# Order of a product, output stores and operand sums changed in a three-stage attention and feed-forward kernel

## The chip, the core and the metric

The kernel runs on one core of a Trainium2 chip. The metric is the device time of one execution in microseconds, lower is better. The engines of the core are named as in the profile: PE (TensorE; PEld is its weight load), DVE (VectorE), ACT (ScalarE), POOL (GpSimd) and SP (SyncE, which here only issues DMAs).

## The reference

Three stages follow one another; all arithmetic is fp32, and the weights arrive as fp64.

```python
kv  = einsum('bhsd,bhse->bhde', k, v)            # 8 batches, 8 heads, 576 tokens, 64 columns
o   = einsum('bhsd,bhde->bhse', q, kv)
o   = o / sqrt(mean(o * o, -1) + 1e-6) * g_norm
x   = o.transpose(0, 2, 1, 3).reshape(4608, 512)
h   = maximum(maximum(x @ w1, x @ w2), x @ w3)   # 512 x 768 each
x1  = h @ w_out                                  # 768 x 512
g   = s * relu(x1 @ w_in) ** 2 + b               # 512 x 2048
out = g @ w_out2                                 # 2048 x 512
```

## The kernel before

All activations lie transposed, with columns on the partitions and 512 tokens along a tile (N = 512, P = 128). Every fp32 operand of a matmul is split into a rounded high half (`fp32r`) and the rest, and a product is three matmuls: high x high, high x low, low x high. `split` does this: ACT writes the high half, DVE or POOL subtracts.

**First network.** A loop over j = 0 to 8 handles nine tiles of 512 tokens: 512 tokens of each batch, and a ninth tile for the 64 left over in each. In its 18 steps (`g1_part`, G1 = 18) tile j is multiplied by w1, w2 and w3; `g1_out` copies or takes the maximum out of PSUM into six hidden tiles, and `h_split` splits each (the last one on DVE, the others on POOL). Then `g2_mm` multiplies the six hidden tiles by w_out for each of four column blocks n, `g2_out` copies the result out of PSUM (ACT) and stores it to DRAM as `x1d`. The attention for tile j+1 and `x_split` run beside this. The fp64 weights of the second network are turned into fp32 on the way and stored to DRAM as `wd[g]`, g = 0 to 7, four quarter-blocks each (`conv_store`, L197).

**Second network.** Both of its products use Strassen's scheme in Winograd's form: a product of 2 x 2 blocks takes seven products i = 0 to 6, of operands that are sums of blocks. The tokens come in pairs of tiles (four wide pairs, and one narrow pair of 2 x 256 tokens from the ninth tile), in the order 0, 1, 4 (the narrow one), 2, 3. `x1_load` brings a pair into the tiles `xh` and `xl`; `right(q, i)` makes the sums of x on DVE (line 530, names `t`) in temporaries `tmp` and splits the operand into a place of its own (14 places, `XS`); `left(g, i)` does the same for the weights. For each pair, four groups g of seven products follow (`product`, L625, PSUM tiles `ps_a`, `ps_b`, `ps_c`), `combine` takes the results out of PSUM (ACT copies, DVE adds, POOL makes two last sums `r` and `d` per half) and `keep` stores them as `gd`. The results lie in a pool of ten buffers with the tag `s`. In the last pair `left` also makes the operands of w_out (g = 4 to 7) in the places that come free.

**Output network.** H = 0 to 9 are the half-steps of the five pairs: `z_load` reads `gd`, `z_right` finishes sums and splits, `z_product` (L693) multiplies, `z_combine` accumulates. After each pair `put` transposes on DVE (L720) and stores `out` from SP (L725; L729 in the narrow pair, which is the last).

**Order.** Each step is entered by `at(position, function, ...)`; a position is about the time of 12 matmuls. SP's queue, and from position 20 on PE's too, are issued in exactly that order, and an instruction that waits holds all behind it. The order on DVE, ACT and POOL is set when the kernel is built, by a planner with its own estimate of each operation's time and with the positions as priorities; on the chip each of them then runs its list in order. T8 is the start of the ninth tile of the first network, T2 that of the first pair, T4 that of the output network.

## Time and profile before

| | us |
|---|---|
| median of 3 runs | 1494.72 (1493.74 to 1497.67) |
| the profiled execution's own time | 1489.72 |
| its span, first to last instruction | 1487.8 |
| PE busy | 1397.1 |
| DVE, ACT, POOL busy | 985.7, 784.2, 524.9 |
| mean granted TensorE clock | 0.98 of full speed |

The profile shows one execution. Its span is what the views divide; 1.9 us of its time lie around the span. Matmuls are pipelined, so a busy PE is not PE at its peak, and what can be read directly are the stretches in which PE stands idle and what ended them. In the views a group of instructions is written as line, engine, operation, output<-inputs by the program's names, sizes and count; a bracket holds the idle time of the engine in front of it and what ended that. The span falls into the first network with the attention (to 754.4 us), the pairs (to 1116.4) and the output network.

### The profile page before, as it was taken

How to read it: one execution, taken by the hardware profiler on the slowest of the kernel's cores; microseconds unless marked ns; L12 is line 12 of the kernel's file. 1: busy time of each engine (PE TensorE's matmuls, PEld its weight loads, DVE VectorE, ACT ScalarE, POOL GpSimd, SP SyncE). 2: the span in 40 equal slices, each digit the busy share in tenths (PEclk: the TensorE clock that was granted, in tenths of full speed). 3: DMA queues.
4: the chain of work that ended last, by engine and by line, in shares of the span. 5: the costliest groups of instructions: out<-in, count | busy, mean ns of one | idle time of the engine just before them, and what ended most of it. 6: DMA issues, size and time to landing. Idle time of an engine off the chain costs nothing.

```text
span 1487.8 us, 19756 instructions
## 1 busy us (share of the span) xinstructions
PE 1397.1 (94%) x6820; PEld 1143.4 (77%) x6820; DVE 985.7 (66%) x1561; ACT 784.2 (53%) x1393; POOL 524.9 (35%) x381
## 2 busy tenths in 40 slices
PE   5777899999999999999999999899998999999995
PEld 2565687878787878787878788887786888888895
DVE  4999564736363737354475746747887888988885
ACT  4545453535343535333366757766786555555553
POOL 3666443434353525331102223222433414141412
PEclk9889999999999999999999999999999999999998
DMA  9974242536374732313125344352667463646342
GB/s 199 196 192 82 85 74 92 104 127 104 107 110 120 111 108 56 86 36 113 46 106 204 138 165 165 124 194 114 219 225 243 127 201 114 214 136 178 120 133 66
DMA packets 232340, 198.44 MB, mean 133 GB/s; under 512 B 128176, under 2 KB 183472, under 8 KB 230576
## 3 DMA queue, kind: packets, MB, share of 16 engines
q1 hardware_dynamic: 232240, 197.19, 47.8%
q8 instruction: 53, 0.87, 0.3%
q14 instruction: 47, 0.39, 0.1%
HBM read 122.68 MB, written 74.45 MB: 133 GB/s over the span
## 4 chain that ended last, share of the span: by engine, by line
PE 36%; DVE 6%; issue 5%; DMA 4%; ACT 2%; POOL 2%; SPq 0%; DVEq 0%; POOLq 0%; ACTq 0%
PE zs_a L693 12%; PE ps_a L625 6%; PE zs_b L693 6%; PE zs_c L693 3%; PE ps_b L625 3%; PE g L96 1%; PE g L97 1%; PE g L95 1%; PE ps_c L625 1%; DVE cs L530 1%; DMA xl<-x1d 1%; DMA z<-gd 1%; DVE zx L92 1%; POOL d L530 1%; DVE x_q L92 1%
## 5 line engine op out<-in xcount | busy, mean ns | idle before, releaser
L95 PE MATMUL g<-xh,w_w 128*128 128x512 f32 x648 | 259.0, 403 | 5.4 <-ACT xh L91 5.4
L96 PE MATMUL g<-xl,w_w 128*128 128x512 f32 x648 | 258.7, 399 | 0.0
L97 PE MATMUL g<-xh,w_w 128*128 128x512 f32 x648 | 256.9, 397 | 0.0
L91 ACT ACTIVATE zx<-z 128x512 fp32r<-128x512 f32 (+1 forms) x280 | 162.0, 588 | 148.8 <-PE zs_a L693 56.3
L625 PE MATMUL ps_a<-x_q,w_q 128*128 128x512 f32 (+1 forms) x960 | 210.1, 370 | 11.3 <-DVE cs L530 8.4
L693 PE MATMUL zs_a<-zx,w_q 128*128 128x512 f32 (+1 forms) x960 | 203.2, 369 | 0.0
L625 PEld LDWEIGHTS ps_a<-x_q,w_q 128*128 128x128 f32 x960 | 167.4, 188 | 46.0 <-DVE cs L530 11.7
L92 DVE TENSOR_TENSOR zx<-z,zx 128x512 fp32r<-128x512 f32 (+1 forms) x234 | 172.2, 754 | 36.4 <-ACT zx L91 35.9
L693 PEld LDWEIGHTS zs_a<-zx,w_q 128*128 128x128 f32 x960 | 168.7, 189 | 30.4
L530 POOL TENSOR_TENSOR d<-cs,r 128x512 f32<-128x512 f32 (+1 forms) x40 | 59.8, 1503 | 282.7 <-ACT r L646 227.3
L95 PEld LDWEIGHTS g<-xh,w_w 128*128 128x128 f32 x648 | 123.7, 191 | 33.3 <-ACT xh L91 7.1
L97 PEld LDWEIGHTS g<-xh,w_w 128*128 128x128 f32 x648 | 124.4, 192 | 27.9 <-issue 0.5
L96 PEld LDWEIGHTS g<-xl,w_w 128*128 128x128 f32 x648 | 124.5, 192 | 26.5 <-DVE xl L92 0.4
L92 POOL TENSOR_TENSOR zx<-z,zx 128x512 fp32r<-128x512 f32 (+1 forms) x46 | 60.0, 1303 | 210.8 <-ACT zx L91 210.8
L167 POOL TENSOR_TENSOR tr_ctr<-tr_ctr 128x512 int32<-128x512 int32 x42 | 55.9, 1330 | 191.1 <-ACT tr_ctr L160 186.8
L369 DVE TENSOR_TENSOR h<-g,h 128x512 f32<-128x512 f32 x108 | 73.9, 684 | 57.7 <-PE g L97 57.6
L693 PE MATMUL zs_b<-zx,w_q 128*128 128x512 f32 (+1 forms) x480 | 105.6, 374 | 5.2 <-DVE zx L92 4.5
L625 PE MATMUL ps_b<-x_q,w_q 128*128 128x512 f32 (+1 forms) x480 | 105.5, 368 | 0.6 <-ACT cs L635 0.5
L693 PEld LDWEIGHTS zs_b<-zx,w_q 128*128 128x128 f32 x480 | 84.6, 191 | 23.0 <-DVE zx L92 6.8
L625 PEld LDWEIGHTS ps_b<-x_q,w_q 128*128 128x128 f32 x480 | 84.2, 188 | 16.1 <-ACT cs L635 1.0
L96 PE MATMUL g<-h,w_o 128*128 128x512 f32 x216 | 85.6, 396 | 10.1 <-DVE h L92 10.1
L95 PE MATMUL g<-h,w_o 128*128 128x512 f32 x216 | 86.5, 400 | 6.3 <-ACT w_o L91 4.2
(156 smaller groups left out, 2433.4 us busy)
## 6 DMA issues: line engine op xcount, KB each, us to landing
z<-gd SPq DMA_DIRECT2D x64, 512.0 KB, 4.4
gd<-cs SPq DMA_DIRECT2D x96, 256.0 KB, 2.0
z<-gd SPq DMA_DIRECT2D x48, 256.0 KB, 4.1
x1d<-x SPq DMA_DIRECT2D x36, 256.0 KB, 2.8
k<-in_k_dram SPq DMA_DIRECT2D x32, 256.0 KB, 4.7
v<-in_v_dram SPq DMA_DIRECT2D x32, 256.0 KB, 5.1
raw_craw<-in_moe_w_in_dram SPq DMA_DIRECT2D x16, 512.0 KB, 4.2
wd<-tr_ctr SPq DMA_DIRECT2D x32, 256.0 KB, 2.9
```

The costliest lines, as they stand in the source:

```text
L91: act(out=hi, in_=src, func=AF.Copy)
L92: eng.tensor_tensor(out=lo, in0=src, in1=hi.bitcast(F32), op=ALU.subtract)
L95: nc.tensor.matmul(ps, lhsT=w[:, 0, sl], rhs=xh, start=first, stop=False)
L96: nc.tensor.matmul(ps, lhsT=w[:, 0, sl], rhs=xl, start=False, stop=False)
L97: nc.tensor.matmul(ps, lhsT=w[:, 1, sl], rhs=xh, start=False, stop=last)
L167: nc.gpsimd.tensor_tensor(out=t, in0=t, in1=r, op=ALU.add)
L369: nc.vector.tensor_tensor(out=st["h", m], in0=ps, in1=st["h", m], op=ALU.max)
L530: eng.tensor_tensor(out=out, in0=in0, in1=in1, op=op)
L625: nc.tensor.matmul(ps, lhsT=w[:, a, c], rhs=x[:, b_, :n], start=new and k == 0 and e == 0, stop=k == HK - 1 and e == 2, skip_group_check=True)
L693: nc.tensor.matmul(ps, lhsT=w[:, a, c], rhs=x[:, b_, :n], start=new and k_ == 0 and e == 0, stop=k_ == 3 and e == 2, skip_group_check=True)
```

## The change

Seven things are altered together.

1. In the first network, for j of 1 and up, column blocks 0 and 1 each take hidden tiles 0 to 4 first, and tile 5 of both after that.
2. `put` stores 32 rows by 512 columns from all 128 partitions in one DMA, where before it stored 128 columns from 32 partitions. In the narrow pair this is 16 stores of 64 KB where there were 32 of 32 KB, and half of those of the second tile are issued on ACT.
3. The sums of x for a pair are made together by `x_sums`: on DVE for the first pair, on POOL in the middle of the pair before for the others. One of them is written in place over its input.
4. In wide pairs after the first, the low halves of (i, k) = (1, 1), (3, 1), (5, 1) and (6, 1) are made on POOL; for the first two, DVE makes the high half where ACT did.
5. In the narrow pair both k of an operand lie in one place; the operands with k = 1 of the pair behind it are made from position 15 of the narrow pair on, where they came 6 positions ahead of their pair.
6. The Strassen sums of w_out are made in the ninth tile of the first network (`s_load`, `s_sums` on POOL and DVE, `s_store`) and written back to `wd`, which has eight quarter-blocks for them; in the last pair `w_load` brings seven finished quarter-blocks in two parts, where four came, and `left` only splits.
7. `tmp` has 6 buffers for 4, the results 9 for 10; the constants `onesf` and `ones` lie in the attention's pool.

The core of the diff:

```diff
-    wd = [dram.tile([P, 4, N], F32, name=f"wd{n}") for n in range(M2 // 2)]
+    wd = [dram.tile([P, 4 if n < M2 // 4 else 8, N], F32, name=f"wd{n}") for n in range(M2 // 2)]
...
             if j:
-                at(t + G1 + max(n, 0.3), g2_mm, j, n, range(M1))
-            at(t + G1 + n + 1.01 if j else t + G1 + 3 + 0.3 * n, g2_out, j, n)
+                if n < 2:
+                    at(t + G1 + max(n, 0.3), g2_mm, j, n, range(M1 - 1))
+                    at(t + G1 + 1.8 + 0.01 * n, g2_mm, j, n, [M1 - 1])
+                else:
+                    at(t + G1 + n, g2_mm, j, n, range(M1))
+            at(t + G1 + max(n + 1.01, 2.01 + 0.1 * n) if j else t + G1 + 3 + 0.3 * n, g2_out, j, n)
...
-        return p2["pool"].tile([P, N], F32, tag="c", bufs=4, name=nm)
+        return p2["pool"].tile([P, N], F32, tag="c", bufs=6, name=nm)
...
+    def s_load(g):
+        st["sq4", g] = quads = [slot(f"l{6 + i}", f"sq_{g}_{i}", F32) for i in range(2)]
+        for n in range(4):
+            nc.sync.dma_start(out=quads[n // 2][:, n % 2], in_=wd[g][:, QUARTERS[n]])
+
+    def s_sums(g):
+        (a11, a12), (a21, a22) = ((r[:, 0], r[:, 1]) for r in st["sq4", g])
+        tt(nc.gpsimd, a22, a21, add, a22)
+        tt(nc.vector, a21, a11, sub, a21)
+        tt(nc.vector, a11, a22, sub, a11)
+        tt(nc.gpsimd, a12, a12, sub, a11)
+
+    def s_store(g):
+        for n in range(4):
+            nc.sync.dma_start(out=wd[g][:, (2, 6, 1, 4)[n]], in_=st["sq4", g][n // 2][:, n % 2])
+
+    def w_load(g, half):
+        st["wq", g, half] = t_ = base.tile([P, 4, N], F32, tag=("xh", "xl")[half], name=f"wq_{g}_{half}")
+        n = 4 - half
+        nc.sync.dma_start(out=t_[:, :n], in_=wd[g][:, 4 * half:4 * half + n])
...
+    def x_sums(q, k, eng):
+        n = width(q)
+        b11, b12, b21, b22 = (p2["raw", q][c][:, r * HK + k, :n] for r in range(2) for c in range(2))
+        t3, t2, t4 = (tmp(f"t{m}_{q}_{k}")[:, :n] for m in (3, 2, 4))
+        tt(eng, t3, b22, sub, b12)
+        tt(eng, t2, t3, add, b11)
+        tt(eng, t4, b21, sub, t2)
+        tt(eng, b12, b12, sub, b11)
+        p2["t", q, k] = (b11, t3, t2, t4, b12, b21, b22)
+
+    def right(q, i, k):
+        n = width(q)
+        if n == N:
+            x = slot(XS[2 * i + k], f"x_q_{q}_{i}_{k}")
+        else:
+            if k == 0:
+                p2["x2", i] = slot(XS[2 * i], f"x_q_{q}_{i}")
+            x = p2["x2", i][:, :, k * n:(k + 1) * n]
+        p2["x", q, i, k] = x
+        f = p2["t", q, k][i]
+        if n == N and q and (i, k) in ((1, 1), (3, 1)):
+            ts(out=x[:, 0], in0=f, scalar1=1.0, scalar2=None, op0=ALU.mult)
+            nc.gpsimd.tensor_tensor(out=x[:, 1], in0=f, in1=x[:, 0].bitcast(F32), op=ALU.subtract)
+        else:
+            split(x[:, 0], x[:, 1], f, nc.gpsimd if n == N and q and (i, k) in ((5, 1), (6, 1)) else nc.vector)
...
-                s_ = st["cs", i, m] = p2["pool"].tile([P, N], F32, tag="s", bufs=10, name=f"cs_{G}_{i}_{m}")[:, :n]
+                s_ = st["cs", i, m] = p2["pool"].tile([P, N], F32, tag="s", bufs=9, name=f"cs_{G}_{i}_{m}")[:, :n]
...
+        for j in range(4):
             if qq < NQ - 1:
-                r0 = (2 * qq + c) * S + u * P
-                nc.sync.dma_start(out=out[r0:r0 + P, f].rearrange("(b r) f -> r b f", r=32), in_=o[part])
+                r0 = (2 * qq + c) * S + u * P + 32 * j
             else:
-                for e in range(2):
-                    r0 = (4 * c + 2 * u + e) * S + N
-                    nc.sync.dma_start(out=out[r0:r0 + REM, f].rearrange("(b r) f -> r b f", r=32),
-                                      in_=o[part, 2 * e:2 * e + 2])
+                r0 = (4 * c + 2 * u + j // 2) * S + N + 32 * (j % 2)
+            eng = nc.scalar if qq == NQ - 1 and c and j % 2 else nc.sync
+            eng.dma_start(out=out[r0:r0 + 32].rearrange("r (a f) -> a r f", a=4), in_=o[:, j])
...
+    for k_ in range(HK):
+        at(T8 + 19.2 + 0.05 * k_, x_sums, 0, k_, nc.vector)
+    for g in range(4):
+        at(T8 + 0.4 + 3.9 * g, s_load, 4 + g)
+        at(T8 + 1.5 + 3.9 * g, s_sums, 4 + g)
+        at(T8 + 3.6 + 3.9 * g, s_store, 4 + g)
     at(T8 + 18.1, x1_load, 0)
...
-            at(T2 + 28 * (n - 1) + (18 if n == 1 else 8), x1_load, qq)
+            at(T2 + 28 * (n - 1) + (17 if n == 1 else 8), x1_load, qq)
+            early = n and PAIRS[n - 1] == NQ - 1
+            for k_ in (1, 0):
+                at(T2 + 28 * (n - 1) + (18.6 if n == 1 else 11) + (2 if n == 1 else 5) * (1 - k_), x_sums, qq, k_, nc.gpsimd)
             for i in range(7):
-                at(T2 + 28 * n - 6 + i, right, qq, i)
+                for k_ in range(HK):
+                    at(T2 + 28 * (n - 1) + 15 + i if early and k_ else T2 + 28 * n - 6 + i, right, qq, i, k_)
     for g in range(4):
-        at(T4 - 28 + (0.5 + 0.1 * g if g < 2 else 7 * g - 6.7), q_load, 4 + g,
+        at(T4 - 28 + max(0.5, 7 * g - 2.5), w_load, 4 + g, 0)
+        at(T4 - 28 + max(0.6, 7 * g + 0.3), w_load, 4 + g, 1)
```

## Rows read from the trace of the kernel before

**Rows 1.** The page: busy time of each engine.
```profile
PE 1397.1 (94%) x6820; PEld 1143.4 (77%) x6820; DVE 985.7 (66%) x1561; ACT 784.2 (53%) x1393; POOL 524.9 (35%) x381
```

**Rows 2.** Busy time by stage: stretch, length, PE, PEld, DVE, ACT, POOL, PEclk, DMA, GB/s.
```profile
700.00:738.00 38.00, 38.00 (x169) 31.49 (x168) 21.59 (x32) 14.34 (x24) 7.20 (x5) 1.00 0.01 1
754.50:1135.00 380.50, 363.91 (x1730) 302.57 (x1729) 254.91 (x407) 263.42 (x471) 110.33 (x81) 0.99 0.47 174
908.00:957.00 49.00, 43.92 (x336) 41.44 (x336) 29.61 (x63) 36.21 (x84) 14.70 (x16) 1.00 0.48 168
1116.00:1135.00 19.00, 14.29 (x52) 10.53 (x51) 16.25 (x22) 12.22 (x22) 8.02 (x5) 0.87 0.80 302
1135.00:1471.00 336.00, 335.50 (x1629) 283.57 (x1628) 281.45 (x504) 186.12 (x335) 102.10 (x75) 1.00 0.50 149
1471.00:1487.80 16.80, 0.55 (x5) 0.34 (x3) 1.58 (x6) 0.00 (x0) 0.00 (x0) 0.61 0.24 63
```

**Rows 3.** Waits over the whole run: total us, times, longest us.
```profile
PEld g L96 <- DVE h L92: 13.0, 7, 2.8
...
PE g L96 <- DVE h L92: 10.1, 7, 2.4
...
PE ps_a L625 <- DVE cs L530: 8.4, 8, 1.9
```

**Rows 4.** Timeline around one join of the first network, DVE, POOL and PE.
```profile
373.56 5.11 POOL L92 TENSOR_TENSOR xl<-o,xh 128x512 fp32r<-128x512 f32 x3 [5.11 <-ACT xh L91]
375.77 1.77 DVE L92 TENSOR_TENSOR h<-h,h 128x512 fp32r<-128x512 f32 x1
...
377.59 0.50 PE L96 MATMUL g<-h,w_o 128*128 128x512 f32 x1 [1.15 <-DVE h L92]
```

**Rows 5.** The last stores: their issues on SP, then DVE's last transposes.
```profile
L729 SPq DMA_DIRECT2D out_dram<-o x32: 343/425/427, 1470.6 to 1485.0; - x32
...
1470.57 14.90 SPq L729 DMA_DIRECT2D out_dram<-o  x32
...
1471.93 0.88 DVE L720 STREAM_TRANSPOSE o<-xlo 128x128 f32<-128x128 f32 x4
...
L725 SPq DMA_DIRECT2D out_dram<-o x128: 315/444/2125, 1199.8 to 1443.2; - x128
```

**Rows 6.** PE at the end of the first pair: start, us, what, idle before it.
```profile
831.96 1.20 PE L625 MATMUL ps_a<-x_q,w_q 128*128 128x512 f32 x4 [0.83 <-DVE cs L530]
```

**Rows 7.** Groups by line and shape on DVE and POOL: count, busy us, mean ns.
```profile
L530 DVE TENSOR_TENSOR t<-xl,xh 128x512 f32<-128x512 f32 x8 | 5.4, 680 | 0.0
...
L530 POOL TENSOR_TENSOR r<-cs,r 128x512 f32<-128x512 f32 x32 | 43.6, 1370 | 2.7 <-POOL d L530 1.2
```

**Rows 8.** DVE and POOL during the last pair.
```profile
1061.31 8.26 POOL L530 TENSOR_TENSOR d<-cs,r 128x512 f32<-128x512 f32 x2 [13.32 <-ACT r L646]
...
1065.42 0.69 DVE L530 TENSOR_TENSOR s<-wq,s 128x512 f32<-128x512 f32 x1
...
1068.35 0.68 DVE L530 TENSOR_TENSOR cs<-ps_b,cs 128x512 f32<-128x512 f32 x1
```

**Rows 9.** Start of the output network: SP's load, PE's wait.
```profile
1121.15 0.32 SPq L667 DMA_DIRECT2D z<-gd  x1
...
1129.31 2.38 PE L693 MATMUL zs_b<-zx,w_q 128*128 128x512 f32 x6 [3.50 <-DVE zx L92]
```

**Rows 10.** SP's loads and DVE's first sum, last tile of the first network.
```profile
690.30 1.93 SPq L545 DMA_DIRECT2D wq<-wd  x4
738.22 0.32 SPq L584 DMA_DIRECT2D xh<-x1d  x1
...
745.90 1.29 DVE L530 TENSOR_TENSOR t<-xl 128x512 f32<-128x512 f32 x2 [0.90 <-DMA xl<-x1d]
```

**Rows 11.** DMA issues: KB each, median us from issue to landing.
```profile
wd<-tr_ctr SPq DMA_DIRECT2D x32, 256.0 KB, 2.9
...
wq<-wd SPq DMA_DIRECT2D x5, 1024.0 KB, 5.8
```

More of the change, by code (lines that the diff above doesn't have):

```diff
@@ L99, in attention_max_ffn_relu2_ffn @@
     nc.scalar.preload_act_table_set("natural_log_exp_and_others")
-    onesf = base.tile([P, P], F32, name="onesf")
-    nc.vector.memset(onesf, 0.0)
-    for h in range(2):
-        nc.vector.memset(onesf[h * D:(h + 1) * D, h * D:(h + 1) * D], 1.0 / D)
-    ones = base.tile([P, P], F32R, name="ones")
-    nc.vector.tensor_copy(out=ones, in_=onesf)
     eps = base.tile([P, 1], F32, name="eps")
@@ L128, in attention_max_ffn_relu2_ffn @@
     psa = actx.enter_context(tc.tile_pool(name="psa", bufs=1, space=PSUM))
+    onesf = at_.tile([P, P], F32, name="onesf")
+    nc.vector.memset(onesf, 0.0)
+    for h in range(2):
+        nc.vector.memset(onesf[h * D:(h + 1) * D, h * D:(h + 1) * D], 1.0 / D)
+    ones = at_.tile([P, P], F32R, name="ones")
+    nc.vector.tensor_copy(out=ones, in_=onesf)
     kvf = at_.tile([P, NP, P], F32, name="kvf")
@@ L189, in attention_max_ffn_relu2_ffn @@
     wt = {}
+    QUARTERS = (0, 5, 7, 3)
     def conv_split(key, slot, eng):
@@ L196, in conv_store @@
     def conv_store(key):
-        nc.sync.dma_start(out=wd[key[1] // 4][:, key[1] % 4], in_=st.pop(("f32", key)))
+        g, n = divmod(key[1], 4)
+        nc.sync.dma_start(out=wd[g][:, n if g < M2 // 4 else QUARTERS[n]], in_=st.pop(("f32", key)))
     def w1_src(n):
@@ L551, in left @@
     def left(g, i):
+        w = wt["q", g, i] = slot(WS[g % 4][i], f"w_q_{g}_{i}")
+        if g >= M2 // 4:
+            f = st["wq", g, i // 4][:, i % 4]
+            if i not in (3, 4, 5):
+                split(w[:, 0], w[:, 1], f, nc.vector)
+            else:
+                act(out=w[:, 0], in_=f, func=AF.Copy, scale=-1.0)
+                stt(out=w[:, 1], in0=f, scalar=-1.0, in1=w[:, 0].bitcast(F32), op0=ALU.mult, op1=sub)
+            return
         a11, a12, a21, a22 = (quarter(g, n) for n in range(4))
@@ L566, in left @@
         f = s_[{1: 3, 2: 2, 4: 1, 6: 4}[i]] if f is None else f
-        w = wt["q", g, i] = slot(WS[g % 4][i], f"w_q_{g}_{i}")
-        if g < 4 or i not in (3, 4, 5):
-            split(w[:, 0], w[:, 1], f, nc.vector)
-        else:
-            act(out=w[:, 0], in_=f, func=AF.Copy, scale=-1.0)
-            stt(out=w[:, 1], in0=f, scalar=-1.0, in1=w[:, 0].bitcast(F32), op0=ALU.mult, op1=sub)
+        split(w[:, 0], w[:, 1], f, nc.vector)
     def width(q):
@@ L624, in product @@
                 for e, (a, b_) in enumerate(((0, 0), (0, 1), (1, 0))):
-                    nc.tensor.matmul(ps, lhsT=w[:, a, c], rhs=x[:, b_, :n], start=new and k == 0 and e == 0,
+                    nc.tensor.matmul(ps, lhsT=w[:, a, c], rhs=x[:, b_], start=new and k == 0 and e == 0,
                                      stop=k == HK - 1 and e == 2, skip_group_check=True)
@@ L703, in z_combine @@
             if i < 3:
-                s_ = st["cs", i, m] = p2["pool"].tile([P, N], F32, tag="s", bufs=10, name=f"zc_{H}_{i}_{m}")[:, :n]
+                s_ = st["cs", i, m] = p2["pool"].tile([P, N], F32, tag="s", bufs=9, name=f"zc_{H}_{i}_{m}")[:, :n]
                 act(out=s_, in_=ps, func=AF.Copy)
@@ L755, in attention_max_ffn_relu2_ffn @@
         if n:
-            at(T2 + 28 * (n - 1) + (18 if n == 1 else 8), x1_load, qq)
+            at(T2 + 28 * (n - 1) + (17 if n == 1 else 8), x1_load, qq)
+            early = n and PAIRS[n - 1] == NQ - 1
+            for k_ in (1, 0):
+                at(T2 + 28 * (n - 1) + (18.6 if n == 1 else 11) + (2 if n == 1 else 5) * (1 - k_), x_sums, qq, k_, nc.gpsimd)
             for i in range(7):
-                at(T2 + 28 * n - 6 + i, right, qq, i)
+                for k_ in range(HK):
+                    at(T2 + 28 * (n - 1) + 15 + i if early and k_ else T2 + 28 * n - 6 + i, right, qq, i, k_)
     for g in range(4):
-        at(T4 - 28 + (0.5 + 0.1 * g if g < 2 else 7 * g - 6.7), q_load, 4 + g,
-           lambda g=g: [base.tile([P, 4, N], F32, tag=("xh", "xl")[g % 2], name=f"wq_{4 + g}")])
+        at(T4 - 28 + max(0.5, 7 * g - 2.5), w_load, 4 + g, 0)
+        at(T4 - 28 + max(0.6, 7 * g + 0.3), w_load, 4 + g, 1)
         for i in range(7):
```

23 lines of the change are left out of this document (2 added, 21 removed).

## The prediction

> **What bounds the kernel now.** I read the page first, then busy time by stage, then PE's waits, and then the timeline at each wait. The page makes PE the engine to watch: busy for 1397.1 of 1487.8 us [rows 1]. The stages show that most of this cannot move. Of the 336 us in which the output network runs, PE is busy 335.5 [rows 2], and the change leaves the number of matmuls as it is. So only the holes in PE's row can shrink, and the reader is to find three kinds of them.
>
> First, seven joins in the first network: its second product waits for the low half of the last hidden tile, 10.1 us before the matmul and 13.0 us before its weight load [rows 3]. Second, the Strassen pairs with the start of the output network: from 754.5 to 1135 us PE is busy 363.9 of 380.5 us, so 16.6 us are idle; the stretch from 1116 adds 14.3 x (1 - 0.87) = 1.9 us at the lower granted clock [rows 2]. That makes 18.5 us. Third, the tail: 16.8 us after 1471 with 0.55 us of PE work [rows 2]. The 150 us of start-up have holes too, but nothing there is changed beyond the place of a few constants.
>
> **The order of the second product (first network).** In each join PE does five of six hidden tiles for column block 0 and then needs the sixth. Its high half is there; its low half, on DVE, starts at 375.77 and takes 1.77 us, and PE starts again at 377.59 after 1.15 us idle [rows 4]. The change puts the five tiles of block 1 in between, 15 matmuls. At 336 us / 1629 = 0.206 us each (from the output network's row, where a quarter of the work is half as wide, so this is low) [rows 2] that is over 3 us. The longest wait is 2.8 us [rows 3], so all seven go. What is late next is the copy of blocks 0 and 1 out of PSUM, now back to back on ACT; ACT is 53% busy [rows 1] and the next tile's first product needs those buffers only after blocks 2 and 3. Bounds 10.1 and 13.0; I take **-11**.
>
> **The last stores.** PE ends at 1471 and DVE's last transposes at 1471.93 + 0.88 = 1472.8, but SP issues 32 stores of 32 KB from 1470.57 for 14.9 us, 0.47 us apiece, and the kernel ends 2.3 us behind the last [rows 5]. The DMA engines are 24% busy there [rows 2]: the issue is the limit. Afterwards there are 16 stores of 64 KB, 12 on SP and 4 on ACT, which has nothing left to do. A 64 KB store of the other pairs was issued in 0.44 us, with the step to the next some 0.49 [rows 5]. SP is then done at 1470.57 + 12 x 0.49 = 1476.5, and the end comes 2.3 us behind it, at 1478.8: 1487.8 - 1478.8 = 9.0. If ACT took no load off SP, it would be 16 x 0.49, 2 us less gain; if the first store went out earlier, 1 us more. I take **-9**, bounds -7 and -10. The other 128 stores keep number and size and leave under a full PE.
>
> **Sums of x on POOL, and shared places.** Four pairs lose 8 sums each from DVE, 0.68 us apiece [rows 7], 5.4 us in a wide pair, just where DVE decides: at the end of the first pair PE stands 0.83 us for DVE's read of PSUM [rows 6], and 8.4 us of PE's waits in all have that form [rows 3]. Four of the 14 low halves of a wide pair go to POOL too, and two high halves to DVE. So DVE has 22 x 0.68 = 15 us of operands per pair before, and 10 x 0.68 plus two copies, about 8 us, after. POOL gets 8 + 4 operations at 1.37 us [rows 7], 16 us in a pair of 76, where POOL is now busy 110 of 380 us [rows 2]: it fits. In the narrow pair, which stands idle 5.1 of 49 us [rows 2], half of the next pair's operands can be made a half-pair earlier, since they find free places.
>
> The price is contention. DVE's low half took 1.77 us while POOL ran [rows 4], and an operation of the same kind took 0.68 without it [rows 7]; DVE's read of PSUM took 0.68 during a POOL run [rows 8]. It goes the other way too: two POOL operations took 8.26 us under a row of 0.69 us DVE operations [rows 8], 5.5 us too long. The Trainium skill's GPSIMD Engine Reference, § 1 Specifications, says that GpSimd shares its SBUF interfaces with VectorE and that they contend when a DVE instruction has two SBUF inputs. By that rule moving sums to POOL gives DVE little back and the pair stage would gain nothing (rival B); the trace agrees on the effect, 1.77 against 0.68 us, though not for the operations that read PSUM.
>
> The sums now run around the middle of a pair, when DVE has mostly PSUM work, and only the four low halves fall into the crowded end. I expect 5 of the 6.8 us at pair ends and in the last pair (16.6 - 5.1 - 4.7), and 3 of the narrow pair's 5.1.
>
> **Sums of w_out kept in DRAM.** In the last pair 16 sums leave DVE, 16 x 0.68 = 11 us of its busiest stretch; that is in the 5 us above. The loads grow from 4 to 7 quarter-blocks, 3 MB more in 76 us, with the DMA engines at 0.47 on average [rows 2]: hidden. At the start of the output network PE stood 3.5 us for an operand whose load left SP at 1121.15, behind the stores of the last results [rows 9]. That queue order stays. I expect 2 of 4.7 + 1.9 us.
>
> So the pair stage gives 5 + 3 + 2 = **-10**, bounds 0 and -18.5. One buffer fewer for results (9 for 10) makes a copy out of PSUM wait for POOL's first result sum of the group before; the copy comes three products (3 x 12 x 0.206 = 7.4 us) after the end of that group and the sum is due after about one, so it costs nothing until POOL is some 5 us late. Narrow operands and extra `tmp` buffers cost nothing by themselves.
>
> The sums are made in the last tile of the first network, where DMA is idle (0.01 busy from 700 to 738 us) and DVE is busy 21.6 of 38 us [rows 2]. Four rounds follow one another through two places: load 1 MB, sum, store 1 MB, and SP holds the load of x behind the last round's store. A round takes 5.8 us (load) + 2.9 (store) [rows 11] + 2 x 1.37 + 2 x 0.68 = 4.1 (POOL and DVE by turns) [rows 7] = 12.8 us. The old loads are issued until 692.2 [rows 10]; I put the landing of the first new one two load times (2 x 5.8 us) behind that, at 704. The last sum is done at 704 + 4.1 + 3 x 12.8 = 746.5, and the load of x leaves at about 748 instead of 738.22 [rows 10], 10 us late. Its data then lands at 755.7 instead of 745.9 [rows 10]; eight sums (5.4 us) and two low halves follow, and PE wants the first of these at 757.1, so about 5 us of stall. If store and next load overlap by 3 us a round, the load of x is 1 us late and PE does not notice. I take **+2**, bounds 0 and +5; DVE's sums standing in its queue for late data are inside this, since PE has four PSUM tiles in hand.
>
> **Sum.** -11 - 9 - 10 + 2 = -28, on the profiled execution's 1489.72 us: 1461.7. The median of the runs shown is 1494.72, 5.0 above that execution, so I predict **1467** for a median.
>
> **Rivals.**
> A, the sum above.
> B, contention eats the pair stage: -11 - 9 + 0 + 2 = -18, 1477. For it speak 1.77 against 0.68 us; against it, that PSUM reads are untouched and these are what PE waits for.
> C, all holes of the pair stage close and the rounds are hidden: -11 - 9 - 18.5 = -38.5, 1456. Against it: the queue at the start of the output network is the same.
> D, slower: POOL's four low halves stand at the crowded end of three wide pairs, on the path of products 1, 3, 5 and 6. If DVE's run of operations starves POOL as in [rows 8], each costs up to 5.5 us, 12 x 5.5 = 66, giving 1533. It turns slower by more than 4.5 us when each is late by (28 + 4.5) / 12 = 2.7 us. Against it: one such case in the trace, and the operands are made one product or more ahead.
> E, the rounds through DRAM take 22 us each, 1.7 times the sum of the medians: the last sum is at 704 + 4.1 + 66 = 774, the load of x 38 us late, PE stands some 33 in place of 2, and the result is 1467 + 31 = 1498, no change. Idle DMA engines speak against it.
> F, the new stores don't do what they say, because a store over 128 partitions takes longer to issue or land: -11 - 10 + 2 = -19, 1476. The 64 KB stores of the other pairs speak against it.
>
> **How the numbers follow.** A 0.60, B 0.18, C 0.10, D 0.05, F 0.04, E 0.03. The prediction is A's 1467, with its own range 1460 to 1475. B and F reach to 1477 with some scatter, C to 1456: 1453 to 1482 leaves out D, E and the edges. 0.3% is 4.5 us, about what separates a change from none here. Faster: A, B, C, F, 0.92; same: E, 0.03; slower: D, 0.05.
>
> **What would show it.** Right: no wait of the second product for DVE's low half in seven joins; 12 last stores on SP and 4 on ACT, the end 7 to 8 us behind PE's last matmul; PE's idle time between the first pair and the output network near 8 us; DVE without x sums after the first pair. Wrong: PE standing for POOL's low halves, the first x load leaving SP after 750, or a pair stage with 16 us idle still. The gain would be mis-sized above all by the pair stage, whose order on DVE, POOL and ACT is set by a planner that I can't follow.

## The result and the profile after

The changed kernel takes **1501.62 us** (median of 6 runs, 1500.23 to 1505.21) against 1493.26 us for the kernel before beside it (6 runs): ratio 1.0057, 95% interval 1.0039 to 1.0076. It is slower by 0.57%, where 1467 us was predicted. The profiled execution took 1500.69 us with a span of 1498.9 us, 11.1 us more than the span before.

I cut both spans at the same five matmuls: the ninth tile's first, the first into the bank ps_c in the first and the last group of the pairs, the output network's first, and the last of all. First the kernel before (stretch, length, busy time of PE, PEld, DVE, ACT and POOL, PEclk, DMA, GB/s):

```profile
168.60:689.10 520.50, 510.41 (x2510) 415.91 (x2509) 268.82 (x394) 219.96 (x382) 209.45 (x148) 1.00 0.42 94
689.10:768.10 79.00, 79.00 (x349) 65.23 (x348) 49.85 (x78) 37.29 (x65) 7.20 (x5) 1.00 0.27 94
768.10:1110.90 342.80, 330.92 (x1597) 276.81 (x1596) 224.13 (x363) 237.65 (x425) 102.31 (x76) 1.00 0.45 166
1116.40:1471.60 355.20, 349.94 (x1681) 294.12 (x1679) 297.67 (x527) 197.94 (x356) 110.12 (x80) 0.99 0.52 157
1471.60:1487.80 16.20, 0.00 (x0) 0.00 (x0) 1.21 (x6) 0.00 (x0) 0.00 (x0) 0.60 0.25 63
```

The same view of the kernel after, which answers to [rows 2], with its page's busy times ([rows 1]) ahead of it:

```profile
PE 1407.1 (94%) x6820; PEld 1151.2 (77%) x6820; DVE 986.6 (66%) x1515; ACT 781.3 (52%) x1387; POOL 592.5 (40%) x433
...
168.60:676.50 507.90, 507.90 (x2513) 417.17 (x2512) 267.91 (x394) 220.60 (x383) 210.52 (x148) 1.00 0.42 96
676.50:769.10 92.60, 84.92 (x350) 67.89 (x349) 57.83 (x84) 35.25 (x64) 18.35 (x13) 0.94 0.50 171
769.10:1118.20 349.10, 336.33 (x1598) 280.06 (x1597) 216.53 (x311) 237.27 (x421) 155.34 (x120) 0.99 0.48 173
1123.60:1484.20 360.60, 350.87 (x1681) 294.93 (x1679) 299.26 (x526) 197.33 (x355) 110.98 (x80) 0.99 0.47 154
1484.20:1498.90 14.70, 0.01 (x1) 0.00 (x0) 1.27 (x6) 0.00 (x0) 0.00 (x0) 0.66 0.25 71
```

The ninth tile starts 12.6 us earlier. Then the kernel loses 13.6 us in the ninth tile, 6.3 in the pairs and 5.4 in the output network, and the tail gives back 1.5 of the 9 forecast: -12.6 + 13.6 + 6.3 + 5.4 - 1.5 = +11.2 (the last tenth is rounding).

PE runs the same 6820 matmuls, but is busy for 10.0 us more of the span. Of the 13.6 us in the ninth tile 7.7 are idle time and 5.9 longer matmuls; of the 6.3 in the pairs it is 0.9 (11.9 us idle before, 12.8 after) and 5.4; of the 5.4 in the output network 4.5 and 0.9. The trace's record of the granted clock tells why matmuls take longer: it has 10.2 us at the lower of the two levels (0.50, 1.2 GHz) in the ninth tile and 10.2 in the pairs, where before there was none in either. At half speed 10.2 us hold the work of 5.1 (an estimate). Each of its four stretches begins inside one of PE's waits or 0.4 us behind its end. Two of them (columns as above):

```profile
754.98:761.81 6.83, 6.16 (x14) 4.38 (x15) 6.30 (x11) 4.29 (x9) 0.00 (x0) 0.50 0.35 119
946.13:952.96 6.83, 5.35 (x25) 5.35 (x26) 6.53 (x10) 2.15 (x4) 6.83 (x7) 0.50 0.11 40
```

**The joins are gone.** From 168.6 to 676.5 us PE is busy for all 507.9 us; the wait of [rows 3] is down to a single one of 0.2 us.

**The ninth tile.** SP's queue and POOL's sums of w_out (start, us, what, idle before it and its releaser):

```profile
679.70 2.99 SPq L559 DMA_DIRECT2D sq<-wd  x4
...
736.25 2.69 SPq L570 DMA_DIRECT2D wd<-sq  x4
739.04 0.39 SPq L618 DMA_DIRECT2D xh<-x1d  x1
...
691.41 1.70 POOL L536 TENSOR_TENSOR sq<-sq 128x512 f32<-128x512 f32 x1 [0.60 <-DMA sq<-wd]
706.87 1.29 POOL L536 TENSOR_TENSOR sq<-sq 128x512 f32<-128x512 f32 x1 [6.74 <-DMA sq<-wd]
720.25 1.29 POOL L536 TENSOR_TENSOR sq<-sq 128x512 f32<-128x512 f32 x1 [4.62 <-DMA sq<-wd]
733.51 1.26 POOL L536 TENSOR_TENSOR sq<-sq 128x512 f32<-128x512 f32 x1 [5.93 <-DMA sq<-wd]
```

From the second round on a round takes 13.3 us, and the load of x stands behind the last store: it leaves 739.0 - 676.5 = 62.5 us into the tile, where before it left at 738.22 - 689.1 = 49.1 [rows 10]. DVE has its own share of each round and stands in line for POOL, and PE pays twice:

```profile
734.81 1.42 DVE L536 TENSOR_TENSOR sq<-sq,sq 128x512 f32<-128x512 f32 x2 [5.47 <-POOL sq L536]
...
737.54 0.50 PE L95 MATMUL g<-h,w_o 128*128 128x512 f32 x1 [4.07 <-ACT h L91]
738.27 0.79 PE L96 MATMUL g<-h,w_o 128*128 128x512 f32 x1 [0.22 <-DVE h L92]
...
755.07 2.08 PE L664 MATMUL ps_b<-x_q,w_q 128*128 128x512 f32 x4 [1.43 <-ACT x L386]
757.73 2.50 PE L664 MATMUL ps_b<-x_q,w_q 128*128 128x512 f32 x5 [0.58 <-DVE x_q L92]
```

Behind each such wait a matmul takes 0.5 to 0.8 us instead of 0.39. The 1.43 us are for a PSUM tile that ACT's copy of x1 (L386) sets free; ACT makes that copy at 754.44, behind the splits of the late x.

**The pairs.** In products 3 to 5 DVE adds PSUM to a copy of an earlier product (L536), which frees the bank, and then squares the result in SBUF (L679). At the end of the first pair POOL is at work on x without a break, and DVE is slow beside it (before: [rows 6]; DVE's and POOL's usual times: [rows 7]):

```profile
819.34 1.74 POOL L536 TENSOR_TENSOR d<-cs,r 128x512 f32<-128x512 f32 x1
821.03 1.47 POOL L536 TENSOR_TENSOR t<-t,xh 128x512 f32<-128x512 f32 x1
...
823.21 3.24 DVE L92 TENSOR_TENSOR x_q<-t,x_q 128x512 fp32r<-128x512 f32 x2 [0.15 <-ACT x_q L91]
826.37 1.27 DVE L536 TENSOR_TENSOR cs<-ps_b,cs 128x512 f32<-128x512 f32 x2
...
827.90 3.45 DVE L679 SCALAR_TENSOR_TENSOR cs<-cs 128x512 f32<-128x512 f32 x2
...
832.01 0.97 PE L664 MATMUL ps_a<-x_q,w_q 128*128 128x512 f32 x3 [2.00 <-DVE cs L536]
...
947.17 0.38 ACT L674 ACTIVATE cs<-ps_a 128x256 f32<-128x256 f32 x1 [1.65 <-POOL d L536]
...
947.61 2.29 PE L664 MATMUL ps_a<-x_q,w_q 128*128 128x256 f32 x9 [3.45 <-ACT cs L674]
```

DVE's instructions with both inputs in SBUF take 1.6 to 1.7 us each (3.24 / 2, 3.45 / 2); the one that reads PSUM keeps its 0.64 (1.27 / 2). PE's wait at the pair's end grew from 0.83 to 2.00 us. In the narrow pair POOL's sum d comes late, ACT waits for the result buffer that it holds, and PE for ACT. Over the pairs as a whole PE waits less for DVE (8.4 us before [rows 3]) and more for ACT's copies; after, and the copies before:

```profile
PE ps_a L664 <- ACT cs L674: 8.0, 9, 3.5
PE ps_a L664 <- DVE cs L536: 4.1, 5, 2.0
...
PE ps_a L625 <- ACT cs L635: 2.8, 5, 1.0
```

**The output network and the stores**, on SP; the answers to [rows 5] are L766's:

```profile
1433.58 23.32 SPq L766 DMA_DIRECT2D out_dram<-o  x32
1456.99 1.11 SPq L709 DMA_DIRECT2D z<-gd  x2
...
1483.00 10.46 SPq L766 DMA_DIRECT2D out_dram<-o  x12
...
1461.87 4.62 PE L732 MATMUL zs_a<-zx,w_q 128*128 128x256 f32 x24 [3.65 <-ACT zx L91]
...
q10 hardware_dynamic: 528, 0.26, 0.1%
```

The last 32 stores of the wide tiles hold SP for 23.3 us, the loads of z behind them leave at 1456.99, and PE stands 3.65 us for an operand made from them. In the tail SP needs 10.46 us for its 12 stores, 0.87 apiece, though one issue takes 0.54 us (min/median/max in ns below): for 3.3 us SP waits for earlier stores to land, three times.

```profile
L766 SPq DMA_DIRECT2D out_dram<-o x12: 536/537/616, 1483.0 to 1492.9; - x12
SPq L766 <- DMA out_dram<-o: 3.3, 3, 1.5
```

By the completions in the trace the last 16 stores land 2.5 to 7.4 us behind their issue, one every 0.83 us from 1485.48 to 1497.95, and the kernel ends 1498.9 - 1493.5 = 5.4 us behind SP's last issue (2.3 before). What limits this tail is the landing, no longer the issue.

The last line of the view before that is the page's row of ACT's queue: 528 packets for four transfers of 64 KB. In pieces of 512 bytes these are 4 x 128 = 512, so 4 more for each transfer; the same bytes in the form of the fifth experiment below leave 576, 16 more for each. In the trace, too, the landing of each of these 16 stores is told by four updates from DMA engines, and that of each of the last stores of the fifth experiment, and of the kernel before, by sixteen. So the changed form seems to run on 4 of the 16 engines. The Trainium skill's DMA: Bandwidth & Descriptors, § Why a DMA increments its semaphore by 16 and not by 1, says that a transfer runs on the largest number of engines, up to 16, that divides the outermost dimension of both its sides: 4 for the changed form, whose DRAM side begins with the four column blocks, and 16 for a side that begins with 32 rows. The packet counts and the updates agree.

### The profile page after: what moved, and what is told of

It is laid out like the page before. It is cut to its first block, busy times and chain, and to the rows that moved or that the text cites. A ratio compares the mean times of both kernels' runs of the same rounds, so it can differ in the third digit from the quotient of the medians.

```text
span 1498.9 us, 19789 instructions
## 1 busy us (share of the span) xinstructions
PE 1407.1 (94%) x6820; PEld 1151.2 (77%) x6820; DVE 986.6 (66%) x1515; ACT 781.3 (52%) x1387; POOL 592.5 (40%) x433
## 5 line engine op out<-in xcount | busy, mean ns | idle before, releaser
L664 PE MATMUL ps_a<-x_q,w_q 128*128 128x512 f32 (+1 forms) x960 | 215.6, 375 | 12.5 <-ACT cs L674 8.0
L664 PEld LDWEIGHTS ps_a<-x_q,w_q 128*128 128x128 f32 x960 | 170.4, 192 | 49.6 <-ACT cs L674 12.3
L92 DVE TENSOR_TENSOR zx<-z,zx 128x512 fp32r<-128x512 f32 (+1 forms) x234 | 173.8, 762 | 38.4 <-ACT zx L91 38.1
L92 POOL TENSOR_TENSOR zx<-z,zx 128x512 fp32r<-128x512 f32 (+1 forms) x46 | 60.1, 1306 | 215.7 <-ACT zx L91 197.1
L536 POOL TENSOR_TENSOR d<-cs,r 128x512 f32<-128x512 f32 (+1 forms) x40 | 51.3, 1292 | 204.9 <-ACT r L685 204.8
L95 PE MATMUL g<-h,w_o 128*128 128x512 f32 x216 | 86.8, 402 | 10.4 <-ACT w_o L91 4.2
L91 ACT ACTIVATE h<-h 128x512 fp32r<-128x512 f32 x54 | 33.9, 629 | 106.2 <-DVE h L371 106.1
```

Of the source, the lines that this page charges most:

```text
L91: act(out=hi, in_=src, func=AF.Copy)
L92: eng.tensor_tensor(out=lo, in0=src, in1=hi.bitcast(F32), op=ALU.subtract)
L95: nc.tensor.matmul(ps, lhsT=w[:, 0, sl], rhs=xh, start=first, stop=False)
L536: eng.tensor_tensor(out=out, in0=in0, in1=in1, op=op)
L664: nc.tensor.matmul(ps, lhsT=w[:, a, c], rhs=x[:, b_], start=new and k == 0 and e == 0, stop=k == HK - 1 and e == 2, skip_group_check=True)
```

## The experiments

Times are medians; the ratio is to the kernel before in the same comparison. The stretches are those above, cut at the same matmuls (with 5.4 us between pairs and output network they add up to the span). In the expectations, "the first pair's third product" is the first one into ps_c, the third PSUM bank, and a pair's step runs from one such matmul to the next.

| kernel | us | ratio, 95% interval | to first ps_c | pairs | output network | tail |
|---|---|---|---|---|---|---|
| before | 1493.26 | | 768.1 | 342.8 | 355.2 | 16.2 |
| after | 1501.62 | 1.0057 (1.0039–1.0076) | 769.1 | 349.1 | 360.6 | 14.7 |
| e1_order | 1477.90 | 0.9906 (0.9888–0.9924) | 755.5 | 343.5 | 353.1 | 16.2 |
| e2_oldput | 1495.07 | 1.0021 (1.0007–1.0034) | 766.0 | 351.7 | 353.8 | 16.2 |
| e3_nosums | 1491.67 | 1.0001 (0.9990–1.0013) | 755.6 | 354.5 | 361.5 | 14.8 |
| e4_dvesums | 1488.44 | 0.9972 (0.9958–0.9985) | 768.7 | 336.3 | 361.7 | 14.6 |
| e5_merged16 | 1486.01 | 0.9956 (0.9937–0.9974) | 774.3 | 344.3 | 354.2 | 7.3 |
| e7_poolsums | 1503.91 | 1.0093 (1.0076–1.0110) | 771.8 | 350.4 | 361.6 | 14.6 |
| e8_bufs9 | 1478.89 | 0.9924 (0.9907–0.9940) | 756.8 | 344.4 | 353.1 | 16.2 |
| e9_halves | 1495.87 | 1.0029 (1.0012–1.0046) | 767.2 | 345.2 | 362.4 | 15.0 |
| e10_round4 | 1489.45 | 0.9982 (0.9968–0.9995) | 758.6 | 349.7 | 361.4 | 14.4 |
| b1_norounds | 1466.55 | 0.9828 (0.9809–0.9847) | 756.4 | 342.8 | 354.2 | 7.2 |
| b2_spread | 1472.16 | 0.9867 (0.9848–0.9886) | 754.2 | 349.9 | 354.2 | 7.0 |
| b3_order_stores | 1468.05 | 0.9837 (0.9818–0.9856) | 756.3 | 345.0 | 353.1 | 7.3 |
| e11_bufs10 | 1497.69 | 1.0034 (1.0018–1.0051) | 764.6 | 348.7 | 360.0 | 14.9 |
| b4_norounds_10 | 1465.67 | 0.9820 (0.9793–0.9848) | 754.8 | 341.5 | 355.5 | 7.3 |

The first stretch holds the start-up, which differs by some us between executions of the same code: e5 shares all of it with the kernel before and stands at 774.3 where that stands at 768.1. One execution's pair stage carries 2 to 3 us of the same kind: it is 349.1, 351.7 and 350.4 us in the changed kernel, e2 and e7, and 342.8, 343.5, 344.3 and 345.0 in the kernel before, e1, e5 and b3, none of which alters a line of it.

My theory was that the loss is a list of separate prices: the rounds of w_out's sums, the stores, the work on x given to POOL. The first four runs take one part each.

**e1: the order of the second product alone**, in the kernel before.

```
             if j:
-                at(t + G1 + max(n, 0.3), g2_mm, j, n, range(M1))
-            at(t + G1 + n + 1.01 if j else ..., g2_out, j, n)
+                if n < 2:
+                    at(t + G1 + max(n, 0.3), g2_mm, j, n, range(M1 - 1))
+                    at(t + G1 + 1.8 + 0.01 * n, g2_mm, j, n, [M1 - 1])
+                else:
+                    at(t + G1 + n, g2_mm, j, n, range(M1))
+            at(t + G1 + max(n + 1.01, 2.01 + 0.1 * n) if j else ..., g2_out, j, n)
```

> The kernel before with one part of the change alone: the new order of the second product in the first network. Theory of separate prices: the seven joins are closed and nothing after the ninth tile's start moves, so the time falls by the 11 to 12.5 us by which the changed kernel's ninth tile started earlier, to about 1482 us. Rival, that the earlier start is given back by itself (the weights' conversion or the loads of x are what sets the ninth tile): under 4 us of it are left, 1489 us or more.

Measured: 1477.9 us, 0.94% less. The order keeps what it gains; the rival falls.

**e2: the old stores** in the changed kernel (`put` of before).

```
-            eng.dma_start(out=out[r0:r0 + 32].rearrange("r (a f) -> a r f", a=4), in_=o[:, j])
+                nc.sync.dma_start(out=out[r0:r0 + P, f].rearrange("(b r) f -> r b f", r=32), in_=o[part])
```

> The changed kernel with the output stores of before (64 KB over 32 partitions, and 32 KB for the narrow tile). Theory of slow issues: the changed stores take 0.64 to 0.87 us of SP's queue each against 0.44 to 0.49, hold SP before two z loads of the narrow tile and leave TensorE about 5 us behind; with the old form those 5 to 7 us come back, and the tail behind TensorE's last product returns to its 16.4 us (from 14.85), so about 1501.6 - 6 + 1.6 = 1497 us. Rival, that the issue time is hidden (the z loads wait for their buffers and not for SP): only the tail changes and the time is 1503 us.

Measured: 1495.07 us. SP's queue in the same place as above:

```profile
1433.38 17.16 SPq L764 DMA_DIRECT2D out_dram<-o  x32
1450.64 0.93 SPq L709 DMA_DIRECT2D z<-gd  x2
```

17.2 us for the same 32 stores instead of 23.3, the loads of z leave 6.4 us earlier, PE's wait of 3.65 us is gone and the output network is back at 353.8 us. The issue time isn't hidden.

**e3: no sums of w_out in DRAM** (no `s_load`, `s_sums`, `s_store`; `left` and `q_load` of before).

```
-        at(T8 + 0.4 + 3.9 * g, s_load, 4 + g)
-        at(T8 + 1.5 + 3.9 * g, s_sums, 4 + g)
-        at(T8 + 3.6 + 3.9 * g, s_store, 4 + g)
-        at(T4 - 28 + max(0.5, 7 * g - 2.5), w_load, 4 + g, 0)
-        at(T4 - 28 + max(0.6, 7 * g + 0.3), w_load, 4 + g, 1)
+        at(T4 - 28 + (0.5 + 0.1 * g if g < 2 else 7 * g - 6.7), q_load, 4 + g, ...)
```

> The changed kernel without the sums of w_out kept in DRAM: their four rounds of loads, sums and stores in the ninth tile are gone, and the sums are made in the last pair as before. Theory that the rounds cost the ninth tile its 13.5 us (x of the first pair asked for 13.3 us later, DVE held by POOL's sums): the stretch from the ninth tile's start to the first pair's third product goes back from 92.5 to about 80 us and the time falls to about 1488 to 1490 us. Rival, that the first pair's start is late for another reason (its sums of x made as one block on DVE): 1499 us or more.

Measured: 1491.67 us. The stretch to the first ps_c falls by 13.5 us, as expected. The time falls by less, since the sums return to the last pair: the pair stage takes 354.5 instead of 349.1 us. So the rounds cost 13.5 and bring 5.4, of which 4.8 stand in the last pair itself (63.0 against 58.2 us for its last three steps).

**e4: the work on x back from POOL.**

```
-            ... x_sums, qq, k_, nc.gpsimd)
+            ... x_sums, qq, k_, nc.vector)
-        if n == N and q and (i, k) in ((1, 1), (3, 1)):
-            ts(out=x[:, 0], ...); nc.gpsimd.tensor_tensor(out=x[:, 1], ...)
-        else:
-            split(x[:, 0], x[:, 1], f, nc.gpsimd if ... in ((5, 1), (6, 1)) else nc.vector)
+        split(x[:, 0], x[:, 1], f, nc.vector)
```

> The changed kernel with the sums of x on DVE for all pairs, and the four low and high halves moved to POOL and DVE put back on DVE and ACT. Theory that POOL's work on x is what makes the pair stage longer (POOL's results late in the narrow pair, DVE slowed beside POOL): the stretch from the first pair's third product to the last step's falls from 349.1 to about 343 us, and the time to about 1495 us. Rival, that the nine result buffers and the narrow pair's shared places alone make those gaps: the gaps stay and the time is 1500 us or more, or DVE is now the late one and the time grows.

Measured: 1488.44 us, and the pair stage takes 336.3 us: 12.8 less than in the changed kernel and 6.5 less than before. The theory had the sign right and half the size. At the end of the first pair, where the changed kernel had 3.45 us for two and PE's wait of 2.00:

```profile
813.10 0.69 DVE L536 TENSOR_TENSOR t<-t,xh 128x512 f32<-128x512 f32 x1
...
817.45 1.78 DVE L536 TENSOR_TENSOR t<-xh,t 128x512 f32<-128x512 f32 x1
...
828.48 0.68 DVE L675 SCALAR_TENSOR_TENSOR cs<-cs 128x512 f32<-128x512 f32 x1
...
831.02 5.05 PE L660 MATMUL ps_a<-x_q,w_q 128*128 128x512 f32 x21 [0.23 <-DVE cs L536]
```

The sums are made by DVE, mostly in 0.69 us each (the one of 1.78 runs beside a sum of POOL's that starts at 816.90), in the place that the change gave them, 10 us and more ahead of the next pair. Step by step, the 6.5 us against before are 1.6 at the end of the first pair (20.0 for 21.6), 2.4 at the end of the fourth (19.2 for 21.6), 0.5 in the narrow pair and 2.3 in the last pair (57.1 for 59.4), less 0.3 elsewhere. The two pair ends come with sums that stand earlier, not with POOL. The 2.3 come with w_out's sums being elsewhere, and with those back in the last pair (b1 below) the stage is 342.8 us, that of before. Inside the narrow pair the last step gains 2.3 us (16.9 for 19.3) and the third loses 2.0 (14.1 for 12.1); what the shared places and what the early sums do there was not separated.

**e5: the last stores merged in another form**, in the kernel before: 64 KB each, 12 on SP and 4 on ACT, but from 32 partitions with the rows outermost (the narrow tile's blocks are transposed in an order that lets four images go in one transfer).

```
-                for e in range(2):
-                    r0 = (4 * c + 2 * u + e) * S + N
-                    nc.sync.dma_start(out=out[r0:r0 + REM, f].rearrange("(b r) f -> r b f", r=32),
-                                      in_=o[part, 2 * e:2 * e + 2])
+                r0 = N + 32 * u
+                dst = out.rearrange("(t s) f -> s t f", s=S)[r0:r0 + 32, 4 * c:4 * c + 4, f]
+                (nc.scalar if c and a % 2 else nc.sync).dma_start(out=dst, in_=o[part])
```

> The kernel before, whose narrow tile is now stored with 16 transfers of 64 KB as in the changed kernel, four of them on ACT, but each from 32 partitions (row, image, features) and not from 128. Theory that the changed stores are slow by their form and not by their number: these take 0.44 to 0.49 us each to issue, the 12 on SP 5.5 us, and the tail behind TensorE's last product falls from 16.2 to about 8.5 us: 7 to 8 us less than before. Rival, that 64 KB takes twice the issue time of 32 KB whatever its form: the tail stays at 14 us or more and the time within 2 us of before.

Measured: 1486.01 us, ratio 0.9956. The tail is 7.3 us, 8.9 less; the execution profiled had 6 us more in its first stretch, in code that is the same. The stores:

```profile
1477.24 5.84 SPq L732 DMA_DIRECT2D out_dram<-o  x12
...
L732 SPq DMA_DIRECT2D out_dram<-o x12: 342/442/553, 1477.2 to 1482.6; - x12
DMA to landing us min/median/max: 1.7/1.9/2.4
...
q10 hardware_dynamic: 576, 0.26, 0.1%
```

0.49 us apiece, and the 16 land one every 0.36 us: the number of stores was right, their form was the loss. With e1's order under them the same stores bring 9.9 us by the medians (b3 below, 1468.05 against 1477.90).

**e7: all four sums of a round on POOL.**

```
-        tt(nc.vector, a21, a11, sub, a21)
-        tt(nc.vector, a11, a22, sub, a11)
+        tt(nc.gpsimd, a21, a11, sub, a21)
+        tt(nc.gpsimd, a11, a22, sub, a11)
```

> The changed kernel with all four sums of a round of w_out on POOL, so that DVE has no instruction that waits for POOL or for the rounds' loads. Theory that DVE, held 4.5 to 5.5 us per round, is what stops TensorE in the ninth tile: the wait of 4.1 us at 737.5 and the half clock behind it go, some 5 to 6 us, but the rounds become longer by one or two of POOL's sums (1.3 us each), so that x of the first pair comes no earlier; about 1495 to 1497 us. Rival, that the rounds cost only by the late load of x: TensorE loses the same at x instead, and the time is 1500 us or more.

Measured: 1503.91 us. The theory that DVE's standing in line is the cost falls. PE's 4.07 us behind `h` are gone, but the load of x leaves at 742.75, 3.7 us later than in the changed kernel, and PE pays there:

```profile
742.75 0.40 SPq L618 DMA_DIRECT2D xh<-x1d  x1
...
749.46 5.79 PE L664 MATMUL ps_a<-x_q,w_q 128*128 128x512 f32 x12 [6.66 <-ACT x_q L91]
```

**e8: nine result buffers**, in e1's kernel: `tag="s", bufs=10` becomes `bufs=9` in both places.

> The kernel before with the new order of the second product (as in the first experiment, 1477.9 us) and nine result buffers where it has ten. Theory that the nine alone cost nothing as long as POOL isn't late: 1477 to 1479 us, and the narrow pair's steps stay at 10.8 to 12.1 us. Rival, that the ninth buffer is what stops ACT in the narrow pair: its third step grows from 11.8 to some 14 us, and the time to 1480 us or more.

Measured: 1478.89 us against e1's 1477.9, with overlapping intervals; the narrow pair's third step takes 12.2 us instead of 11.8. Alone it costs nothing that can be told.

**e9: the halves back, the sums still on POOL** (the second part of e4's diff alone).

> The changed kernel with the four halves of x that went to POOL and DVE put back on DVE and ACT, the sums of x still on POOL. With the sums of x on DVE as well it took 1488.4 us, 12 us less than the changed kernel. If POOL's sums cost it: under 3 us of the 12 come back, 1497 us or more, and the first pair's end keeps its 24.2 us. If the halves cost it: 9 us or more come back, 1491 us or less, and that step falls to about 20 us.

Measured: 1495.87 us, between the two: the pairs take 345.2 us. In these executions the halves account for 3.9 of the 12.8 us and the sums for 8.9; by the medians it is 5.8 and 7.4. The places agree: the first pair's last step keeps 23.8 us (24.2 in the changed kernel, 20.0 in e4), and the narrow pair its 70.8 (70.8 and 67.4), as POOL's sums should have it, while the fourth pair's last step (22.1 to 19.2) and the last pair (58.2 to 57.1) come back with the halves alone.

**e10: the fourth round elsewhere**: made in the second pair, in a buffer of x.

```
-    for g in range(4):
+    at(T2 + 29, s_load, 7, "xl")
+    at(T2 + 31.2, s_sums, 7)
+    at(T2 + 34.2, s_store, 7)
+    for g in range(3):
         at(T8 + 0.4 + 3.9 * g, s_load, 4 + g)
```

> The changed kernel with its fourth round of w_out's sums moved out of the ninth tile into the second pair (its quarters then stand in a buffer of x). Theory of the late load: three rounds of 13.3 us fit before the moment at which x's buffers come free (49 us behind the ninth tile's start), so x is asked for at that moment again and nearly all of the 13.5 us come back: first pair's third product at about 757 us of the span, 1488 to 1491 us. Rival, that each round costs by itself (DVE held, SP's queue): a quarter of it comes back, 3 to 4 us, and the time is 1496 us or more.

Measured: 1489.45 us. Three rounds, and the load of x:

```profile
724.67 2.91 SPq L571 DMA_DIRECT2D wd<-sq  x4
728.35 0.32 SPq L619 DMA_DIRECT2D xh<-x1d  x1
```

It leaves 10.7 us earlier, PE's waits at 737 and 752 to 758 us are gone (one of 1.26 us is left, at 725), and 758.6 us are reached instead of 769.1. The cost is a step: with three rounds the load of x leaves 50.7 us into the tile (728.35 - 677.6, where this tile begins), near the 49.1 of before, and the fourth is what costs over 10 us. Its ninth tile has no stretch at the lower clock. In all 16 kernels the first ps_c comes 27.2 to 30.2 us behind the load of x, whether that leaves 49 or 66 us into the tile: the load had next to no slack. In the five with the change's own ninth tile (the changed kernel, e2, e4, e9, e11) it leaves 61.6 to 63.0 us into the tile, and the tile takes 9.9 to 13.9 us more than the 78.9 of the kernels without rounds.

**b1, b2, b3: putting together.** b1 has the order, the narrow pair's shared places, all work on x on DVE, no rounds, and e5's stores. b2 adds the rounds in the first three pairs, all on POOL. b3 is the kernel before with the order and e5's stores alone.

```
# b2, against b1
+    for g, (n, a) in enumerate(((0, 1), (1, 0), (1, 1), (2, 1))):
+        t = T2 + 28 * n
+        at(t + 1.0, s_load, 4 + g, ("xh", "xl")[a])
+        at(t + 3.2 + 0.1 * a, s_sums, 4 + g)
+        at(t + 6.2 + 0.1 * a, s_store, 4 + g)
```

> Put together from the runs: the new order of the second product, the narrow pair's shared places, the sums of x and all low halves on DVE, no sums of w_out in DRAM, and the narrow tile stored with 16 transfers over 32 partitions. If the prices add: 755.5 us to the first pair's third product (first experiment), some 341 for the pair stage (336.3 and the last pair's own 4.5), 5.4, 353.1 for the output network and a tail of 7.3, so a span of 1462 and a time of about 1464 us. Rival, that the parts hinder each other: above 1470 us.

> As the last, but with w_out's sums kept in DRAM and their four rounds made in the first three pairs, all on POOL, in the buffers of x. If POOL and SP have room there: the pair stage takes 336 to 338 us and the time is about 1459 us. Rival, that the rounds hold SP's stores of the results or the loads of x: pair steps of 20 us or more come back and the time is 1464 us or more.

> The kernel before with the new order of the second product and the 16 transfers over 32 partitions, and nothing else. If the two add: 1477.9 - 8.9 = 1469 us. If the last pair's end or the stores of the wide tiles set the end instead: 1473 us or more.

Measured: 1466.55, 1472.16 and 1468.05 us. The prices add in b1 and b3, within 3 us. b1 and b3 can't be told apart by their intervals: all that b1 has beyond the order and the stores is worth about 1.5 us. Its last pair shows why: it takes 63.2 us, 3.8 more than before, and so eats the 4.0 that its two pair ends gain; PE waits there 3.2 us for DVE. In b2 the prices don't add: the pairs take 349.9 us, 13.6 more than e4's 336.3. PE waits 8.5 us there for ACT's copies:

```profile
PE ps_a L660 <- ACT cs L670: 8.5, 7, 3.0
```

The rival written before the run fits: SP stands 11.8 us in line for POOL's sums (L570), the stores of the results leave behind that, and ACT waits 5.1 us for these stores to give their buffers back, which b1's pairs show nowhere. The rounds cost as much in the pairs as they did in the ninth tile, and more than the 6.1 us that they save in the last pair (b1's two last steps, 23.4 + 20.8, against 2 x 19.04).

**e11 and b4: ten result buffers** and five places for sums, in the changed kernel and in b1 (`tag="s", bufs=10`; `tag="c", bufs=5`).

> The changed kernel with ten result buffers again (and five places for sums where it has six). Theory that the missing tenth buffer passes POOL's lateness on to ACT: ACT's wait of 1.6 us for POOL in the narrow pair goes, its third step falls from 16.9 to about 14 us, and the time by 2 to 3 us. Rival, that POOL's late sums stop TensorE by themselves: the step stays at 16 us or more and the time within 2 us of the changed kernel.

> The fastest kernel so far (1466.55 us: new order, shared places, all sums on DVE, none kept in DRAM, stores over 32 partitions) with ten result buffers and five places for sums. If the ninth buffer limits the narrow pair even with an idle POOL: its third step falls from 14.3 to 12 us and the time to about 1464 us. If not: 1466 us, or more if five places for sums hold DVE in the last pair.

Measured: 1497.69 and 1465.67 us. In e11 the third step falls from 16.9 to 13.7 us, as the theory has it, but the next one grows from 12.6 to 15.4: from the narrow pair's beginning to the wide one's first step it is 69.9 us instead of 70.8 (68.0 before, 67.4 in e4). The missing buffer decides where POOL's lateness reaches PE, not how much of it. What lowered e11 by 4 us stands mostly in its first stretch (its ninth tile takes 88.8 us for 92.5) and isn't explained; e2's, written the same, takes 89.8. b4 can't be told from b1.

## Why the prediction was wrong, point by point

**The order, -11: right.** -12.6 in the trace and 0.94% (14 us) by itself in e1.

**The rounds, +2: the first step that failed.** The cycle was right, 12.8 us worked out against 13.3 measured, and so was the first landing (15 us into the tile). The load of x came 13.4 us late where I had 10. My own sum then gave 5 us of stall, as if the load had 5 us of slack; I took 2 on the chance that stores and loads overlap, gave the lower clock no price, and wrote that DVE's standing in line was covered by PE's four PSUM tiles. It cost 13.6: PE stood idle for 7.7 us, for `h` and then for x, and 5.9 went into longer matmuls, with 10.2 us at the lower clock. e7 shows that the two waits replace each other, and e10 and the steady 27 to 30 us from the load to the first ps_c that the late load is what sets them. Rival E described this mechanism with 33 us and had 0.03.

**The pair stage, -10: the second.** It came out at +6.3. Rival B was right that contention eats the gain, and too mild. I had exempted what decides at the pair's end because it reads PSUM; but the step there is two instructions, and the second (L679) has both inputs in SBUF: 1.73 us beside POOL. In the sum I also put the lower clock and sums of POOL's that come late at nothing. PE's waits for DVE did fall, from 8.4 to 4.1 us, but those for ACT's copies, behind POOL in the narrow pair, grew from 2.8 to 8.0, and 5.4 of the 6.3 us are longer matmuls. With the same sums, as early, on DVE (e4), the stage gives -6.5, near the 8 that I had for it without the start of the output network. That the sums are so close is in part luck: the pair ends and the last pair give 6.3 of that where I had 5, the narrow pair 0.5 where I had 3, and 2.3 of the 6.3 hang on the rounds, which cost more elsewhere. The rule from the Trainium skill's GPSIMD Engine Reference, § 1 Specifications, quoted in the prediction, spoke for rival B. The trace agrees with it for L92 and L679, and the PSUM reads keep 0.64 us. To rival D, POOL's halves, e9 assigns 3.9 us (5.8 by the medians).

**Sums of w_out off the last pair, inside the pair stage's 5 us: right in kind, smaller than it looks.** It is 4.8 to 6.1 us in kernels that have x's sums early (e3, b1's last steps), but the last pair of before took 59.4 us, and on that the gain is 2.3.

**The start of the output network, -2: nothing came.** PE's wait there is 4.07 us (3.50 before [rows 9]).

**Nine buffers, 0: right alone** (e8); the condition that I named, POOL late, came true, and e11 shows that it only moves the wait.

**The last stores, -9: the third.** The number and the split were right, and e5 gives 8.9 us with them. The failed step is that the issue is the limit, at 0.49 us a store with the end 2.3 us behind the last: I read both from stores of another form. In the changed form the landing is the limit: SP needs 10.46 us where I had 5.9, 3.3 of them waiting for landings, and the end comes 5.4 us behind. This was rival F, with 0.04. I also wrote that the other 128 stores "keep number and size and leave under a full PE"; they cost the output network's 5.4 us, because SP's queue holds the loads of z behind them.

**Sum.** With the measured terms -12.6 + 13.6 + 6.3 + 5.4 - 1.5 = +11.2 in the profiled executions; +8.4 by the medians.

## What to carry to other kernels

When work moves to another queue, ask what stands behind its last instruction: every engine had room for the rounds, and they cost 13 us because one load stood behind the fourth store. Price a DMA by its form, not its size; a store whose outermost dimension is small landed later here and held the issuing queue longer, and that queue may hold loads that PE needs. Before giving work to POOL, try the same work earlier on the engine that has it: here the pair stage was 12.8 us shorter that way than with POOL. Price a wait of PE with what follows it at the lower clock. And weigh the parts against each other: the order of one product and the form of the last stores (b3, 1468.05) alone came within 2.4 us of the fastest kernel here (b4, 1465.67).
